# RWKV attention and SwiGLU block on one core: sign bits from the PSUM copy, a later third weights load, and units 2 and 3 in another order

## The chip, the cores and the metric

The kernel runs on one core of one Trainium2 chip. The metric is the time of one execution on the device in microseconds (us). The engines are PE (TensorE, matrix products), ACT (ScalarE), DVE (VectorE), POOL (GpSimd) and SP (SyncE, which issues most transfers). Each works through its own queue in order, and they wait for one another through semaphores. SBUF is the memory that engines and transfers share; PSUM is the small memory that PE writes its results into[...].

## The reference, cut to what matters

```
for t in range(S):                                   # rwkv5, B=4, H=8, S=768, D=48
    y[:, :, t] = r_t @ (state + u * k_t (x) v_t)
    state = w * state + k_t (x) v_t
x = y.transpose(0, 2, 1, 3).reshape(B * S, H * D)     # 3072 x 384
out = (silu(x @ w_gate) * (x @ w_val)) @ w_out        # d_ff = 1536
```

Here (x) is the outer product of a key and a value. The three weight matrices come in as 64-bit floats; everything else is fp32. The kernel therefore has to turn the weights into fp32 itself, by bit operations.

## The kernel before, in words

**Units.** The sequence is cut in 6 chunks of 128 steps. A chunk of one of the 4 batches is a unit, so there are 24 units; units 0 to 3 are the first chunks of the four batches. Within a unit the recurrence is a masked product of scores with v, plus a product with the state Z that came out of the earlier chunks.

A unit passes through these steps. `load(i)` brings k and r, `load_v(i)` brings v. `own_product(i)` and `own_sum(i)` (POOL, then DVE) form the diagonal term `du`. `turn(i)` transposes k and r on PE into a PSUM tile `tp`, and DVE (units 0 to 3, multiplying by a table of powers of w) or ACT (later units) copies it out as `kT` and `rT`. `diagonal(i)` writes `du` on the diagonal of `At`: four or eight blocks on ACT, the rest on POOL. `scores(i)` multiplies kT with rT on PE and DVE copies the part above the diagonal into `At` (COPY_PREDICATED, L386). `outputs(i)` forms `y_ps` on PE from At and v (and from Z, when the unit is not in the first chunk), and ACT copies it to `xT`. `update(i)` multiplies the scaled keys (`khat`, scaled by `scale_k` on POOL) with v on PE; for the first chunk DVE multiplies the result by w to the 128th, `w128`, into Z (L436).

**The block after it.** `gate_value(g, f)` computes 128 columns of the gate and of the value product for two units at a time: six matrix products into one PSUM tile `gv` (L450), the sigmoid on ACT (L456), and two products on DVE (L457, L458), the second of which writes `hT` and frees `gv`. There are two `gv` tiles. `project` multiplies hT with w_out. From the third pair of units on, other routines do both products with fewer matrix products; the change does not touch them.

**Weights.** They come in 18 chunks of 128 x 768 numbers, 768 KB each, in the order gate, value, gate, value, ..., then out. `load_weights` fetches the next chunk into one of three buffers `w_bits`; a number is a high and a low 32-bit word side by side. Rounding a chunk takes two halves. For each half, ACT reads the high words as fp32, takes the absolute value times 2 to the -112 (which moves the exponent) and writes it to PSUM as `w_mag` (`round_high`, L173). For the whole chunk ACT also scales the low words into `w_low` (`round_low`, L179; two buffers). DVE then does two operations for each half (`round_dve`): L188 takes the sign bit from the high words into the weight tile, and L189 shifts `w_mag` left by three and ORs it in. Last, POOL adds `w_low` (L199 for the halves of the first two chunks, L218 for whole chunks after that). `w_mag` has two places, `ps_w` and `ps_o`, one PSUM bank each, so a half can be prepared on ACT while DVE works on the other.

**What sets the order.** The program's order is the order of every engine's queue; nothing reorders it. The first part, units 0 to 3, is written out by hand after `flush()`; a loop over units from 4 on follows, with weights (`R`) and pieces of the feed-forward block (`F`) placed by the table `EARLY`. `feed(1)` emits the next piece whose weights are done. PSUM tiles of the attention part share four places (`ps_a`), taken in turn: a new tile waits until the tile four places before it has been read out. SP issues loads in the program's order too, and a load waits until the old contents of its buffer have been read.

Of the kernel before, what the change touches and what calls it, by code (L numbers as in the profile page):

```python
# [9 lines left out]
FP32 = mybir.dt.float32  # L10
INT32 = mybir.dt.int32
UINT32 = mybir.dt.uint32
AF = mybir.ActivationFunctionType
ALU = mybir.AluOpType
# [8 lines left out]
def fast(  # L23
# [44 lines left out]
    dve, pool, act, pe, sp = nc.vector, nc.gpsimd, nc.scalar, nc.tensor, nc.sync  # L68
# [6 lines left out]
    w128 = cst.tile([P, HP], FP32, name="w128")  # L75
# [41 lines left out]
    def load_v(i):  # L117
        c, b = divmod(i, B)
        rows = slice(P * c, P * (c + 1))
        for e in range(2):  # L120
            sp.dma_start(
                out=v_ld[i % 4][:, :, 64 * e : 64 * e + D],
                in_=v[b, :, rows, :].rearrange("(a e) t d -> e t a d", e=2)[e],
            )
# [14 lines left out]
    bits, mags, lows = {}, {}, {}  # L139
    done = {"load": 0, "act": 0, "pool": 0}  # L140

    def next_chunk(stage):
        n = done[stage]
        done[stage] = min(n + 1, NW)
        return n if n < NW else None

    def load_weights():
        n = next_chunk("load")
        if n is not None:
            src = chunks[n][0].bitcast(INT32)  # L150
            bits[n] = three.tile([P, WN, 2], INT32, name="w_bits", tag="w_bits")
            sp.dma_start(
                out=bits[n][:].rearrange("p (c f) two -> p c (f two)", c=src.shape[1]), in_=src
            )
# [6 lines left out]
    def halves(x, n):  # L161

        c = chunks[n][1].shape[1]
        x = x.rearrange("p (c f) -> p c f", c=c)
        f = x.shape[2]
        return [x[:, :, 0 : f // 2], x[:, :, f // 2 : f]] if c == 3 else [x[:, 0:1], x[:, 1:2]]

    def round_high(n, half, bank):
        hi = halves(bits[n][:, :, 1], n)[half]
        ps, tag = ((ps_w, "w_mag"), (ps_o, "o"))[bank]  # L170
        mag = ps.tile([P, WN // 2], INT32, name="w_mag", tag=tag)
        mags[n, half] = mag[:].rearrange("p (c f) -> p c f", c=hi.shape[1])
        act.activation(  # L173
            mags[n, half].bitcast(FP32), hi.bitcast(FP32), AF.Abs, scale=float(2.0**-112)
        )

    def round_low(n):
# [3 lines left out]
        )  # L181

    def round_dve(n, half):
        hi = halves(bits[n][:, :, 1], n)[half]
        f = hi.shape[2]
        dst = chunks[n][1].bitcast(INT32)
        dst = dst[:, :, half * f : half * f + f] if hi.shape[1] == 3 else dst[:, half : half + 1]
        dve.tensor_scalar(dst, hi, -(1 << 31), None, ALU.bitwise_and)  # L188
        dve.scalar_tensor_tensor(  # L189
            dst, mags.pop((n, half)), 3, dst, ALU.logical_shift_left, ALU.bitwise_or  # L190
        )

    def add_low(n, half):

        dst = chunks[n][1].bitcast(INT32)
        f = dst.shape[2] // 2
        cols = slice(half * f, half * f + f)
        low = lows[n][:].rearrange("p (c f) -> p c f", c=dst.shape[1])
        pool.tensor_tensor(dst[:, :, cols], dst[:, :, cols], low[:, :, cols], ALU.add)  # L199

    def round_act(next_load=1):
        n = next_chunk("act")
        if n is not None:
            round_high(n, 0, 0)
            round_low(n)
            round_dve(n, 0)
            round_high(n, 1, 1)
            round_dve(n, 1)
            del bits[n]
            for _ in range(next_load):  # L210
                load_weights()
# [15 lines left out]
    def own_product(i):  # L227
        kl, rl = raw(i)
        rk = two.tile([P, H, D], FP32, name="rk", tag="rk")[:]
        pool.tensor_mul(rk, rl, kl)  # L230
        pool.tensor_mul(rk, rk, ub[:])
        rks[i] = rk

    def own_sum(i):
        dus[i] = three.tile([P, H], FP32, name="du", tag="du")
        dve.tensor_reduce(dus[i][:], rks.pop(i), axis=AX.X, op=ALU.add)  # L236
# [39 lines left out]
    pw, pv = tables[:, 0, :, 0 : P + 1], tables[:, 1, :, 0:P]  # L276
    dve.memset(pw[:, :, P : P + 1], 1.0)
    dve.tensor_copy(pw[:, :, P - 1 : P], held[:].unsqueeze(2))
    for l in range(7):
        n = 1 << l  # L280
# [19 lines left out]
    def scale_k(i):  # L300
        pool.tensor_mul(khat[i % 4][:, :, 0:D], raw(i)[0], kscale[:])
# [4 lines left out]
    def natural_tables():  # L306
        for t, dst in ((pw[:, :, 1 : P + 1], kscale), (pv, rscale)):
            t_ps = ps_a.tile([P, HP, P], FP32, name="t_ps", tag="a")
            for a in range(HP):
                pe.transpose(t_ps[:, a, :], t[:, a, :], ident[:])  # L310
            act.copy(dst[:], t_ps[:].rearrange("p a (e x) -> p (a e) x", e=2)[:, :, 0:D])
# [5 lines left out]
    def diagonal(i):  # L317

        du = dus.pop(i)
        on_act = HP if i < 4 else H  # L320
        small.extend(
            lambda h=h: act.activation(  # L322
                At[i % 2][:, h, :], ident[:], AF.Identity, scale=du[:, h : h + 1]
            )
            for h in range(on_act)
        )
        if on_act < H:
            n = H - on_act
            pool.tensor_mul(
                At[i % 2][:, on_act:H], ident[:].unsqueeze(1).to_broadcast([P, n, P]),  # L330
                du[:, on_act:H].unsqueeze(2).to_broadcast([P, n, P]),
            )
# [4 lines left out]
    def turn(i):  # L337
        kr = khat[i % 4], rhat_of(i)
        tps = [ps_a.tile([P, HP, P], FP32, name="tp", tag="a") for _ in kr]
        turned[i] = three.tile([P, HP, P], FP32, name="rT", tag="rT")  # L340
        for tp, t, dst, table in zip(tps, kr, (kT[i % 2], turned[i]), (pw[:, :, 1 : P + 1], pv)):
            for a in range(HP):
                pe.transpose(tp[:, a, :], pair(t, a), ident[:])
            if i < 4:
                dve.tensor_mul(dst[:], tp[:], table)
            else:
                act.copy(dst[:], tp[:])
# [27 lines left out]
    def scores(i):  # L375

        ps = [ps_a.tile([P, HP, P], FP32, name="s_ps", tag="a") for _ in range(2)]
        for a in range(HP):
            for e in range(2):
                rows = slice(64 * e, 64 * e + D)  # L380
                pe.matmul(  # L381
                    ps[e][:, a, :], kT[i % 2][rows, at(i, a), :], turned[i][rows, at(i, a), :],
                    start=True, stop=True, skip_group_check=True,
                )
        for e in range(2):
            dve.copy_predicated(  # L386
                At[i % 2][:].rearrange("p (a e) t -> p a e t", e=2)[:, :, e],
                mask[:].bitcast(INT32).unsqueeze(1).to_broadcast([P, HP, P]), ps[e][:],
            )
# [27 lines left out]
    def update(i):  # L417
        c, b = divmod(i, B)
        if c == NCH - 1:
            return  # L420
        kh, vl, z = khat[i % 4], v_ld[i % 4], Z[b]
        ps = ps_a.tile([P, HP, D], FP32, name="u_ps", tag="a")
        for a in range(HP):
            for q in range(4):
                e, half = divmod(q, 2)
                pe.matmul(  # L426
                    ps[32 * q : 32 * q + 32, a, :], kh[:, 2 * a + e, 32 * half : 32 * half + 32],
                    vl[:, a, 64 * e : 64 * e + D],
                    start=True, stop=True, skip_group_check=True,
                )  # L430
        for e in range(2):
            rows = slice(64 * e, 64 * e + D)
            ze = z[rows, :, D * e : D * e + D]
            w = w128[rows].unsqueeze(2).to_broadcast([D, HP, D])
            if c == 0:
                dve.tensor_mul(ze, ps[rows], w)  # L436
            else:
                dve.tensor_add(ze, ps[rows], ze)
                pool.tensor_mul(ze, ze, w)
# [289 lines left out]

    turn(0)  # L730
    natural_tables()
    own_sum(0)
    diagonal(0)
    flush()
    own_product(1)
    load(2)
    load_weights()
    load_v(2)
    warm(3)
    turn(1)  # L740
    load(3)
    load_v(3)
    scores(0)
    own_sum(1)
    diagonal(1)
# [17 lines left out]
    for n in range(2):  # L763
        round_high(n, 1, n)
        round_dve(n, 1)
        add_low(n, 1)
        del bits[n], lows[n]
    done.update(act=2, pool=2)
    load_weights()
    turn(2)  # L770
    feed(1)
    own_sum(2)
    diagonal(2)
    flush()
    own_product(3)
    turn(3)
    dve.tensor_copy(w128[:].unsqueeze(2), pw[:, :, 0:1])
    scores(2)
    update(0)
    update(1)  # L780
    own_sum(3)
    diagonal(3)
    flush()
    scores(3)
    scale_k(2)
    outputs(2)
    load(4)
    round_act()
    feed(1)
    outputs(3)  # L790
    scale_k(3)
    round_act()
    round_pool()
    scale(4)
    load_v(4)
    feed(1)
    update(2)
    update(3)
    round_pool()
    own_product(4)  # L800
    load(5)
# [464 lines left out]
```

## Time and profile before

The median of 3 runs is 629.39 us (628.95 to 630.25). The profiled execution has a span of 627.9 us, with a PE clock of 1.00 in every stretch.

| what | us |
|---|---|
| span | 627.9 |
| PE busy | 611.4 |
| DVE busy | 366.8 |
| POOL busy | 300.1 |
| ACT busy | 239.5 |
| last rounding of weights on DVE starts | 104.8 |
| one L188 on DVE, shortest and longest | 0.35, 1.96 |
| one L189 on DVE | 0.56 |
| one L173 on ACT, median | 0.53 |

Busy time is an average over the whole span. A queue that is full in one stretch only is seen in the forty slices of the page (a digit is the busy share of a slice in tenths) and in the busy times by stretch. Who waited for whom is read from the list of waits, and when, from the order of time, where the number in brackets is the idle time ahead of an instruction and the name in it is what ended that idle time. "x" counts instructions; matrix products appear twice in these counts, since one fp32 product is run as two.

### The profile page before, as it was taken

The numbers are of one execution on the slowest core, as the hardware profiler recorded it, in microseconds if no ns is written. First come the engines' busy times: TensorE is split into PE (matmuls) and PEld (weight loads), VectorE is DVE, ScalarE is ACT, GpSimd is POOL, SyncE is SP. The second block draws the span as 40 slices with busy tenths as digits, with TensorE's granted clock in tenths as the row PEclk, the third lists the DMA queues.
The fourth block names the chain that finished last, engine by engine and source line by source line (L and its number), as shares of the span: only waits on it lengthen the run. The fifth ranks groups of instructions, "written<-read, shape, count | busy, mean of one in ns | idle before, by whom it ended". The sixth has DMA issues, their size and how long they took to land.

```text
span 627.9 us, 13037 instructions
## 1 busy us (share of the span) xinstructions
PE 611.4 (97%) x5040; PEld 550.5 (88%) x5040; DVE 366.8 (58%) x751; ACT 239.5 (38%) x647; POOL 300.1 (48%) x350
## 2 busy tenths in 40 slices
PE   8799999999999999999999999999999999999996
PEld 7588778899888899988899888899988899988896
DVE  6889999465556563466566355665345453355460
ACT  3368777321353512245330435432253321233310
POOL 5789778946648413563543635441433211443110
PEclk9999999999999999999999999999999999999999
DMA  8979873244341203322222402121000000000001
GB/s 191 246 169 243 219 242 94 40 72 80 73 69 24 45 12 66 76 47 45 40 37 57 92 12 37 25 42 41 27 2 1 1 1 26 27 0 1 1 2 55
DMA packets 138007, 40.47 MB, mean 64 GB/s; under 512 B 128592, under 2 KB 131792, under 8 KB 137936
## 3 DMA queue, kind: packets, MB, share of 16 engines
q1 hardware_dynamic: 134480, 34.82, 26.5%
q10 hardware_dynamic: 3456, 4.72, 2.1%
q8 instruction: 42, 0.69, 0.5%
q14 instruction: 29, 0.24, 0.1%
HBM read 28.51 MB, written 4.72 MB: 53 GB/s over the span
## 4 chain that ended last, share of the span: by engine, by line
PE 86%; DVE 7%; ACT 2%; DMA 2%; issue 1%; POOL 0%; DVEq 0%; ACTq 0%; POOLq 0%
PE c_b L627 25%; PE c_a L627 21%; PE o_f L521 13%; PE o_a L521 8%; PE o_b L521 6%; PE y_ps L411 5%; PE gv L450 4%; PE s_ps L381 3%; DVE At L386 1%; PE warm L265 1%; DMA hats<-in_r_dram 1%; DMA w_bits<-in_moe_w_out_dram 1%; DVE wg L188 1%; DVE wo L188 1%; PE u_ps L426 1%
## 5 line engine op out<-in xcount | busy, mean ns | idle before, releaser
L611 POOL TENSOR_TENSOR hT<-hT,u 128x256 f32<-128x256 f32 x60 | 46.9, 782 | 149.0 <-DVE hT L610 121.8
L634 ACT COPY u<-c_a 128x256 f32<-128x256 f32 x120 | 44.5, 371 | 85.8 <-PE c_a L627 83.5
L627 PE MATMUL c_a<-t,wv 128*128 128x256 f32 x240 | 72.0, 382 | 0.1
L627 PE MATMUL c_b<-xT,wg 128*128 128x256 f32 x240 | 71.6, 380 | 0.0
L607 ACT ACTIVATE sg<-hT 128x256 f32<-128x256 f32 x120 | 50.1, 417 | 52.5 <-DVE hT L636 33.8
L322 ACT ACTIVATE At<-ident,du 128x128 f32<-128x128 f32 x176 | 62.1, 398 | 16.2 <-DVE du L236 7.3
L627 PE MATMUL c_b<-xT,s 128*128 128x256 f32 x240 | 61.6, 379 | 0.0
L641 DVE TENSOR_TENSOR u<-u,c_b 128x256 f32<-128x256 f32 x60 | 25.1, 418 | 60.5 <-PE c_b L627 55.4
L627 PEld LDWEIGHTS c_b<-xT,s 128*128 128x128 f32 x240 | 45.2, 190 | 6.6 <-DVE u L641 0.2
L627 PEld LDWEIGHTS c_a<-t,wv 128*128 128x128 f32 x240 | 44.9, 190 | 6.9 <-ACT u L634 1.1
L627 PEld LDWEIGHTS c_b<-xT,wg 128*128 128x128 f32 x240 | 45.3, 190 | 6.0
L636 DVE TENSOR_TENSOR hT<-p,c_b 128x256 f32<-128x256 f32 x60 | 25.1, 419 | 41.6 <-PE c_b L627 38.6
L587 POOL TENSOR_TENSOR s<-wv,wg 128x256 f32<-128x256 f32 x24 | 17.6, 733 | 65.5 <-PE o_f L521 50.8
L386 DVE COPY_PREDICATED At<-mask,s_ps 128x512 f32<-128x512 int32 x48 | 32.9, 741 | 19.9 <-PE s_ps L381 12.4
L450 PE MATMUL gv<-xT,wg 128*128 128x256 f32 x144 | 36.9, 392 | 3.1 <-DVE hT L458 2.5
L304 POOL TENSOR_TENSOR hats<-r_ld,rscale 128x384 f32<-128x384 f32 x20 | 20.9, 1045 | 36.1 <-DMA v_ld<-in_v_dram 19.0
L639 DVE TENSOR_TENSOR hT<-hT,c_a 128x256 f32<-128x256 f32 x60 | 25.3, 421 | 19.8 <-PE c_a L627 18.4
L643 DVE TENSOR_TENSOR hT<-u,c_b 128x256 f32<-128x256 f32 x60 | 25.2, 421 | 19.8 <-PE c_b L627 19.6
L627 PE MATMUL c_b<-t,s 128*128 128x256 f32 x120 | 36.2, 383 | 0.3 <-DVE hT L636 0.3
L411 PE MATMUL y_ps<-At,v_ld 128*32 128x128 f32 x768 | 34.9, 273 | 1.4 <-DVE At L386 1.4
L627 PE MATMUL c_b<-xT,wv 128*128 128x256 f32 x120 | 35.9, 381 | 0.0
L627 PE MATMUL c_a<-t,s 128*128 128x256 f32 x120 | 35.8, 380 | 0.0
(135 smaller groups left out, 1394.6 us busy)
## 6 DMA issues: line engine op xcount, KB each, us to landing
hats<-hats SPq DMA_DIRECT2D x192, 32.0 KB, 2.0
w_bits<-in_moe_w_gate_dram SPq DMA_DIRECT2D x6, 768.0 KB, 6.5
v_ld<-in_v_dram SPq DMA_DIRECT2D x48, 96.0 KB, 3.4
w_bits<-in_moe_w_val_dram SPq DMA_DIRECT2D x6, 768.0 KB, 5.9
w_bits<-in_moe_w_out_dram SPq DMA_DIRECT2D x6, 768.0 KB, 6.0
out_dram<-o_sb ACTq DMA_DIRECT2D x24, 192.0 KB, 1.9
k_ld<-in_k_dram SPq DMA_DIRECT2D x20, 192.0 KB, 3.1
r_ld<-in_r_dram SPq DMA_DIRECT2D x20, 192.0 KB, 3.9
```

What stands on the lines that cost most here:

```text
L322: lambda h=h: act.activation(At[i % 2][:, h, :], ident[:], AF.Identity, scale=du[:, h : h + 1])
L386: dve.copy_predicated(At[i % 2][:].rearrange("p (a e) t -> p a e t", e=2)[:, :, e], mask[:].bitcast(INT32).unsqueeze(1).to_broadcast([P, H ...
L411: pe.matmul(ps[32 * q : 32 * q + 32, cc, :], *x, start=start, stop=stop, skip_group_check=True,)
L450: pe.matmul(gv[:, o, :].rearrange("p (i t) -> p i t", i=2), wt[:, c, P * f : P * (f + 1)], xT[:, 2 * g % NX : 2 * g % NX + 2, c, :], start ...
L521: pe.matmul(ps, lhs[:, f, :], rhs[:, f, :], start=(f == 0 and n in (0, 1, 4)), stop=(f == FH - 1), skip_group_check=True,)
L607: act.activation(x[what, f][:], h[j], AF.Sigmoid)
L611: pool.tensor_mul(h[1], h[1], x.pop(("u3", f))[:])
L627: pe.matmul(ps.rearrange("p (i t) -> p i t", i=2), lhs, rhs, start=first, stop=what not in ("p2", "p5", "p4", "p3"), skip_group_check=True,)
L634: act.copy(x[nm, f][:], ps)
L636: dve.tensor_add(h[0], x.pop(("p1", f))[:], ps)
L639: dve.tensor_mul(h[0], h[0], ps)
L643: dve.tensor_add(h[1], x.pop(("u2", f))[:], ps)
```

## The change

It has three parts.

1. The sign bit comes from PSUM. ACT copies the high words with their sign (`AF.Copy` in place of `AF.Abs`), so `w_mag` holds the sign as well, and both DVE operations read it. DVE no longer reads `w_bits`. Its purpose is to take one read of SBUF from DVE; in return the first of the two operations now has to wait for ACT's copy.
2. The third chunk of weights is fetched after k, r and v of unit 3 instead of ahead of v of unit 2, so that the unit's inputs come first.
3. The work of units 2 and 3 is put in another order. `turn(2)`, its diagonal, scores and `outputs(2)` come earlier, `turn(3)` comes after the scores of unit 2 and the updates of units 0 and 1, and the updates of units 2 and 3 stand right after `outputs(3)`. The copy of `w128` moves to the start, where the table of powers has just been made.

```
@@ round_high
         act.activation(
-            mags[n, half].bitcast(FP32), hi.bitcast(FP32), AF.Abs, scale=float(2.0**-112)
+            mags[n, half].bitcast(FP32), hi.bitcast(FP32), AF.Copy, scale=float(2.0**-112)
         )
@@ round_dve
-        hi = halves(bits[n][:, :, 1], n)[half]
+        hi = mags.pop((n, half))
...
         dve.tensor_scalar(dst, hi, -(1 << 31), None, ALU.bitwise_and)
-        dve.scalar_tensor_tensor(
-            dst, mags.pop((n, half)), 3, dst, ALU.logical_shift_left, ALU.bitwise_or
-        )
+        dve.scalar_tensor_tensor(dst, hi, 3, dst, ALU.logical_shift_left, ALU.bitwise_or)
@@ the order by hand
     natural_tables()
+    dve.tensor_copy(w128[:].unsqueeze(2), pw[:, :, 0:1])
     own_sum(0)
...
     load(2)
-    load_weights()
     load_v(2)
     warm(3)
     turn(1)
     load(3)
     load_v(3)
+    load_weights()
     scores(0)
...
         round_dve(n, 1)
+    turn(2)
+    own_sum(2)
+    diagonal(2)
+    for n in range(2):
         add_low(n, 1)
         del bits[n], lows[n]
     done.update(act=2, pool=2)
     load_weights()
-    turn(2)
     feed(1)
-    own_sum(2)
-    diagonal(2)
     flush()
-    own_product(3)
-    turn(3)
-    dve.tensor_copy(w128[:].unsqueeze(2), pw[:, :, 0:1])
     scores(2)
     update(0)
     update(1)
+    own_product(3)
+    turn(3)
+    outputs(2)
     own_sum(3)
     diagonal(3)
     flush()
     scores(3)
     scale_k(2)
-    outputs(2)
     load(4)
     round_act()
     feed(1)
     outputs(3)
     scale_k(3)
+    update(2)
+    update(3)
     round_act()
     round_pool()
     scale(4)
     load_v(4)
     feed(1)
-    update(2)
-    update(3)
     round_pool()
```

More of the change, by code (lines that the diff above doesn't have):

```diff
@@ L173, in round_high @@
         act.activation(
-            mags[n, half].bitcast(FP32), hi.bitcast(FP32), AF.Abs, scale=float(2.0**-112)
+            mags[n, half].bitcast(FP32), hi.bitcast(FP32), AF.Copy, scale=float(2.0**-112)
         )
@@ L183, in round_dve @@
     def round_dve(n, half):
-        hi = halves(bits[n][:, :, 1], n)[half]
+        hi = mags.pop((n, half))
         f = hi.shape[2]
@@ L188, in round_dve @@
         dve.tensor_scalar(dst, hi, -(1 << 31), None, ALU.bitwise_and)
-        dve.scalar_tensor_tensor(
-            dst, mags.pop((n, half)), 3, dst, ALU.logical_shift_left, ALU.bitwise_or
-        )
+        dve.scalar_tensor_tensor(dst, hi, 3, dst, ALU.logical_shift_left, ALU.bitwise_or)
     def add_low(n, half):
@@ L731, in fast @@
     natural_tables()
+    dve.tensor_copy(w128[:].unsqueeze(2), pw[:, :, 0:1])
     own_sum(0)
@@ L736, in fast @@
     load(2)
-    load_weights()
     load_v(2)
@@ L742, in fast @@
     load_v(3)
+    load_weights()
     scores(0)
@@ L765, in fast @@
         round_dve(n, 1)
+    turn(2)
+    own_sum(2)
+    diagonal(2)
+    for n in range(2):
         add_low(n, 1)
@@ L769, in fast @@
     load_weights()
-    turn(2)
     feed(1)
-    own_sum(2)
-    diagonal(2)
     flush()
-    own_product(3)
-    turn(3)
-    dve.tensor_copy(w128[:].unsqueeze(2), pw[:, :, 0:1])
     scores(2)
@@ L780, in fast @@
     update(1)
+    own_product(3)
+    turn(3)
+    outputs(2)
     own_sum(3)
@@ L785, in fast @@
     scale_k(2)
-    outputs(2)
     load(4)
@@ L791, in fast @@
     scale_k(3)
+    update(2)
+    update(3)
     round_act()
@@ L796, in fast @@
     feed(1)
-    update(2)
-    update(3)
     round_pool()
```

## The prediction, made before the changed kernel had run

> **What bounds the kernel now.** First the page: busy times and the forty slices.
>
> ```profile
> PE 611.4 (97%) x5040; PEld 550.5 (88%) x5040; DVE 366.8 (58%) x751; ACT 239.5 (38%) x647; POOL 300.1 (48%) x350
> PE   8799999999999999999999999999999999999996
> DVE  6889999465556563466566355665345453355460
> ```
>
> TensorE (PE) is busy nearly throughout, so the change can only win back PE's idle time: 627.9 - 611.4 = 16.5 us. VectorE (DVE) is full only in the first seven slices, where the weights are rounded. Next, what PE waited for from 9 to 110 us (columns: line, who ended the wait, us in total, times, longest):
>
> ```profile
> PE gv L450 <- DVE hT L458: 2.5, 3, 1.1
> PE y_ps L411 <- DVE At L386: 1.4, 2, 1.2
> PE y_ps L411 <- ACT kT L347: 1.0, 1, 1.0
> PE tp L343 <- DMA hats<-in_k_dram: 1.0, 1, 1.0
> PE tp L343 <- DMA hats<-in_r_dram: 0.8, 2, 0.5
> PE gv L450 <- ACT xT L415: 0.6, 1, 0.6
> PE s_ps L381 <- DVE At L386: 0.5, 1, 0.5
> ```
>
> That is 7.8 us. The same view after 110 us names one wait, 0.3 us: time saved before 110 us should reach the end. PE's order of time puts the three hT waits at 76.66, 90.12 and 102.92 us, the kT wait at 58.66, the DMA waits at 19.98, 24.20 and 25.33, the long At wait at 17.44 and the xT wait at 35.50. Third, the stretches between two outputs on PE (columns: stretch, then busy us and count of PE, PE's loads, DVE, ACT, POOL):
>
> ```profile
> 70.81:84.17 13.36, 12.38 (x150) 10.45 (x149) 12.56 (x24) 9.50 (x23) 10.86 (x10) 1.00 0.75 220
> 84.17:97.63 13.46, 12.38 (x149) 10.45 (x148) 12.32 (x25) 9.77 (x24) 11.08 (x10) 1.00 0.75 224
> ```
>
> A unit costs PE 12.38 us but takes 13.4: DVE sets that pace (92 to 94% busy, the rest almost all gaps between dependent instructions). Fourth, why DVE is slow, in order of time, GpSimd (POOL) first:
>
> ```profile
> 53.58 1.87 POOL L218 TENSOR_TENSOR wv<-wv,w_low 128x768 int32<-128x768 int32 x1
> 54.48 1.26 DVE L188 TENSOR_SCALAR wg<-w_bits 128x384 int32<-128x384 int32 x1
> 55.84 0.56 DVE L189 SCALAR_TENSOR_TENSOR wg<-w_mag,wg 128x384 int32<-128x384 int32 x1
> 56.31 0.41 DVE L188 TENSOR_SCALAR wv<-w_bits 128x384 int32<-128x384 int32 x1
> ```
>
> The first L188 ends 0.29 us after POOL's addition (53.58 + 1.87 = 55.45; 54.48 + 1.26 = 55.74); the second, with POOL idle at its start, takes 0.41. L189, which reads PSUM, takes 0.56 all 36 times. The 36 L188 sum to 28.0 us, mean 0.78; 17 of them are over 0.6.
>
> **What the Trainium skill says.** "SBUF — State Buffer", section Who interferes with whom: VectorE and GpSimd share a pair of SBUF ports, held for a whole instruction; tensor_scalar can take the pair, while an instruction with at most one SBUF input, outside the two-port modes, does not contend. "VectorE: DVE Perf Modes", section Why PSUM operands drop a tier: any PSUM operand caps fp32 at 1x and rules the two-port mode out. The trace agrees: L188 waits POOL out, L189 never does.
>
> **Part 1, the sign from PSUM.** L188 now reads w_mag in PSUM, 384 elements, and should no longer wait for POOL. Its new duration is not in the trace. Below: 0.41, its uncontended time now. Above: 0.56, L189's, same size with a PSUM operand. I take 0.55, because DVE's PSUM operations follow size (256 elements 0.42, 512 elements 0.68; the middle is 0.55). A pair L188+L189 costs duration + 0.10 to the next start + 0.48: before 0.78 + 0.58 = 1.36, after 1.13. From 52 us on the 24 L188 sum to 20.5 us, mean 0.85; after 24 x 0.55 = 13.2, saving 7.3 us of DVE. Per unit: DVE from the At copy at 74.41 to that at 87.88 is 13.47 us with six L188 of 4.81 us and a 0.46 wait; 13.47 - (4.81 - 3.30) - 0.46 = 11.5, under PE's 12.38. So PE sets the pace there and the three hT waits, 2.47 us, go. I leave 0.3 for in-order waits that remain.
>
> The added wait: L188 now waits for ScalarE's copy, where only L189 did. Where ScalarE is late, the 0.65 us from L188 to L189 moves behind it, and the whole DVE queue with it. It bites at 20 us: ScalarE's second-half copies follow xT at 19.50 and 19.97. Now L188 19.37, L189 20.06, kT of unit 2 at 21.53. After: L188 20.00, L189 20.65, L188 21.13, L189 21.78, kT 22.26, so 0.73 later. Copy in place of Abs: the w_mag row has the same size, taken at its 0.53; nothing. The bits buffer is now released by ScalarE's last read instead of DVE's; weight loads can be issued earlier, which only helps.
>
> **Part 2, the load order.** The third chunk (768 KB) goes behind v of unit 2 and k, r, v of unit 3. DMA moved 257 GB/s from 9 to 30 us, so k and r of unit 3 land about 3 us earlier (about 21 and 22 us) and stop mattering. The chunk was issued at 15.63 and will be near 22 or 23; landing took about 7 us, so about 29.5. ScalarE reads it at about 31 (below): hidden, with 1.5 us to spare.
>
> **Part 3, the order around units 2 and 3.** PE after: transposes of unit 2 and the first gate/value product until 23.2 as now; then scores(2), updates 0 and 1, transposes(3), y(2), scores(3). I walk it with trace durations. rT of unit 2 ends 23.5 (PE idles 0.35); scores 23.55 to 24.65; updates to 25.5. The diagonal: the row sum ends 24.0, ScalarE's four At 25.25, POOL's 25.1, so the At copy is 25.3 to 26.6. transposes(3) need its PSUM: 26.0 to 27.2 (idle 0.5). DVE: Z of units 0 and 1 26.6 to 28.0, kT and rT of unit 3 to 29.3. y(2) 27.4 to 28.5 (idle 0.2), scores(3) 29.3 to 30.4 (idle 0.8), gate/value 33.2, y(3) 34.3, updates 2 and 3 35.1, gate/value 35.1 to 37.9 (no xT wait: the updates fill it), next to 40.7. It ends at 41.80 now: 1.1 us gained. The copy of w128 (L777), 1.03 us while POOL works, moves to 10.8 us where POOL is idle and DVE waits anyway (0.67 before kT): nothing.
>
> What reaches the next stage is less. POOL runs without a pause from 35.98 to 55.45 in the trace. It starts when the third chunk's second L189 ends. After: At copy of unit 3 ends at 32.4 (33.3 now), two pairs to 34.7, so POOL starts 1.2 earlier. But Z of units 2 and 3 (1.47) now stand ahead of the fourth chunk's pairs: 34.7 + 0.8 (sg, hT) + 1.47 + 2.26 = 39.2, and POOL's second addition, at 39.85 now, starts at 39.2: 0.6 earlier. From there POOL sets the pace: w_low at 55.48 waits for POOL (its wait is in the trace), kT behind it frees the PSUM of y(4), the wait at 58.66. That wait stays. With some 0.3 from POOL no longer held up by L188 (its 1.82 us additions took up to 2.02), y(4) starts about 0.9 earlier, not 1.1.
>
> **Sum.** 0.9 by 58.66, plus 2.47 - 0.3 = 2.2 from the hT waits: 3.1 us. 629.4 - 3.1 = 626.3.
>
> **Rivals.** (A) POOL and ScalarE take over as the bound. For: POOL has 10.9 us of work in a unit of 12.38, w_low waits for it (1.44 at 75.41, 1.57 at 88.67), and now all of a rounding half waits for ScalarE. Against: POOL's 2.1 to 2.3 us idle once a unit is wait for DVE. If each of three units keeps 0.5: 3.1 + 0.3 - 1.5 = 1.9; with the start at 0.5 instead of 0.9, 1.5: 627.9. (B) More: DVE catches up before 58 us, so that wait goes too (1.0) and the start gives its full 1.1 with no residue (0.5 more): 4.6, so 624.8. Against: POOL's unbroken chain. (C) Slower: L188 is stalled by ScalarE often. With 0.35 us at each of 24 halves a pair is 1.48 against 0.85 + 0.58 = 1.43 now: 1.2 us more DVE where it is the bound; with the start 0.5 later (kT 0.73 late, nothing returned): 631.1. For: the 0.46 wait at 87.41 and that at 20 us. Against: these are the only two waits of L189 for ScalarE, 0.7 us in all, and ScalarE often waits for DVE instead (6.3 us).
>
> **Chances.** Forecast (625.4 to 627.2) 0.54, A (627.2 to 628.6) 0.23, B (below 625.4) 0.13, C and a return of all gains 0.10. Range 624.4 to 628.6: it leaves out C and the end of B. 0.2% is 1.26 us, a limit of 628.1; a little of A lies above it: faster 0.80, same 0.13, slower 0.07.
>
> **What would show it.** L188 all near 0.55, none over 0.7 (right); waits for ScalarE ahead of L188, near 20 us and few later; the hT waits of PE gone, units of 12.4 us between 58 and 110; the kT wait near 58 us still there, with w_low waiting for POOL; no DMA wait ahead of transposes(3). Wrong if L188 still follows POOL's ends, if PE shows new waits for the weights (wg, wv) or for w_low's successors, or if the third chunk lands after 31 us.

## The result, and the profile after

The changed kernel takes 625.9 us (median of 6 runs, 625.04 to 626.39) against 629.24 us before (6 runs); the ratio is 0.9944, with a 95% interval of 0.9931 to 0.9957. Measured twice more beside other kernels it came to 0.9936 (0.9922 to 0.9949) and 0.9937 (0.9923 to 0.9950). The profiled span went from 627.9 to 624.1 us.

Line numbers after the change are two lower than before for most of the code (L448 is the old L450), except L188 and L189, which keep theirs; POOL's long addition L218 is now L216.

First the page after: busy times and slices.

```profile
PE 610.6 (98%) x5040; PEld 550.9 (88%) x5040; DVE 358.1 (57%) x751; ACT 239.4 (38%) x647; POOL 297.3 (48%) x350
PE   8799999999999999999999999999999999999996
DVE  6878996373556574466575355574355463355460
```

DVE lost 8.7 us of busy time (366.8 to 358.1), nearly all of it L188: its 36 instructions take 19.9 us, against 28.0. PE's busy time hardly moved; what went is its idle time. The waits of PE from 9 to 110 us (line, who ended the wait, us in total, times, longest):

```profile
PE s_ps L379 <- DVE rT L343: 1.5, 2, 0.8
PE y_ps L409 <- issue: 1.2, 1, 1.2
PE y_ps L409 <- ACT kT L345: 0.8, 1, 0.8
PE tp L341 <- DVE At L384: 0.4, 1, 0.4
PE tp L341 <- POOL hats L299: 0.4, 1, 0.4
PE tp L341 <- POOL hats L302: 0.3, 1, 0.3
PE y_ps L409 <- DVE At L384: 0.2, 1, 0.2
```

The three waits for hT (2.5 us) are gone, and so are those for transfers (1.8) and for xT (0.6). New are the waits for rT of units 2 and 3 and, near 44.5 us, for POOL's scaling of unit 5. The wait for kT ahead of y of unit 4 shrank from 1.03 to 0.77. Next, two stretches between outputs on PE (stretch, then busy us and count of PE, PE's loads, DVE, ACT, POOL):

```profile
70.23:82.38 12.15, 12.15 (x150) 10.54 (x149) 10.99 (x24) 9.67 (x23) 10.79 (x10) 1.00 0.78 244
82.38:94.52 12.14, 12.14 (x149) 10.53 (x148) 11.47 (x24) 10.17 (x25) 10.50 (x10) 1.00 0.78 244
```

PE is busy without a break and a unit takes 12.15 us, not 13.4. DVE, at 90 to 94% of that, no longer sets the pace. Last, in order of time, an L188 that starts while POOL adds:

```profile
53.17 1.84 POOL L216 TENSOR_TENSOR wv<-wv,w_low 128x768 int32<-128x768 int32 x1
53.34 0.55 DVE L188 TENSOR_SCALAR wg<-w_mag 128x384 int32<-128x384 int32 x1
53.92 0.56 DVE L189 SCALAR_TENSOR_TENSOR wg<-w_mag,wg 128x384 int32<-128x384 int32 x1
```

It ends 1.1 us before POOL does. In the trace before, all 24 of the L188 that took longer than 0.42 us ended 0.21 to 0.29 us after an operation of POOL, and the other 12 took 0.35 to 0.42. After the change, the view of the line L188 (count, then shortest, median and longest in ns) has all 36 near 0.55, and it names the one new wait:

```profile
L188 DVE TENSOR_SCALAR wg<-w_mag x12: 542/547/558, 15.7 to 69.8; 128x384 int32<-128x384 int32 x12
L188 DVE TENSOR_SCALAR wv<-w_mag x12: 532/549/558, 18.2 to 74.5; 128x384 int32<-128x384 int32 x12
L188 DVE TENSOR_SCALAR wo<-w_mag x12: 547/558/559, 77.2 to 98.2; 128x384 int32<-128x384 int32 x12
...
  ACT w_mag L173: 2.5, 5
```

### The profile page after: what moved, and what is told of

Its sections match the earlier page's. It is cut to its first block, busy times and chain, and to the rows that moved or that the text cites. A ratio compares the mean times of both kernels' runs of the same rounds, so it can differ in the third digit from the quotient of the medians.

```text
span 624.1 us, 13011 instructions
## 1 busy us (share of the span) xinstructions
PE 610.6 (98%) x5040; PEld 550.9 (88%) x5040; DVE 358.1 (57%) x751; ACT 239.4 (38%) x647; POOL 297.3 (48%) x350
## 4 chain that ended last, share of the span: by engine, by line
PE 87%; POOL 4%; DVE 3%; SPq 2%; issue 1%; ACT 1%; DMA 1%; ACTq 0%; DVEq 0%; POOLq 0%
PE c_b L625 23%; PE c_a L625 19%; PE o_f L519 13%; PE o_a L519 8%; PE gv L448 7%; PE o_b L519 6%; PE y_ps L409 5%; PE s_ps L379 3%; SPq L356 2%; PE warm L263 1%; PE tp L341 1%; PE u_ps L424 1%; DMA r_ld<-in_r_dram 1%; POOL wv L216 1%; DVE At L384 1%
## 5 line engine op out<-in xcount | busy, mean ns | idle before, releaser
L448 PE MATMUL gv<-xT,wg 128*128 128x256 f32 x144 | 36.6, 390 | 0.0
L625 PE MATMUL c_a<-xT,wg 128*128 128x256 f32 x120 | 35.8, 380 | 0.0
```

Source lines behind the costliest of these rows:

```text
L448: pe.matmul(gv[:, o, :].rearrange("p (i t) -> p i t", i=2), wt[:, c, P * f : P * (f + 1)], xT[:, 2 * g % NX : 2 * g % NX + 2, c, :], start ...
L625: pe.matmul(ps.rearrange("p (i t) -> p i t", i=2), lhs, rhs, start=first, stop=what not in ("p2", "p5", "p4", "p3"), skip_group_check=True,)
```

## The experiments

Twelve runs in three groups of four follow. Each group ran on one chip beside the kernel before, which took 629.82 us in the first, 629.62 in the second and 630.20 in the third; the ratios of a group are to its own value. My theory: the loss was L188 waiting for the SBUF ports that POOL held; part 1 removes it and brings nearly everything; what the order at the start brings is set by POOL's chain. Rivals are named with each test.

**Part 1 alone.** The edit, on the kernel before:

```
-            mags[n, half].bitcast(FP32), hi.bitcast(FP32), AF.Abs, scale=float(2.0**-112)
+            mags[n, half].bitcast(FP32), hi.bitcast(FP32), AF.Copy, scale=float(2.0**-112)
...
-        hi = halves(bits[n][:, :, 1], n)[half]
+        hi = mags.pop((n, half))
```

> Part 1 alone: the sign from ScalarE's copy in PSUM, with the load order and the order of units 2 and 3 of before. Theory (part 1 carries nearly all): L188 at 0.55 us, units on PE of 12.15 us from 58 us on, the three hT waits of PE gone, about 3.2 us; at the start the late kT of unit 2 hides behind the wait for k and r of unit 3, so another 0.2 to 0.4. Time about 625.8, that is 3.4 us under the kernel before. Rival (the order is needed for it): with the old order DVE stays behind, two of three hT waits remain, and the time is about 628.

Measured: 625.93 us, ratio 0.9936 (0.9922 to 0.9949), which can't be told from the whole change (0.9936 to 0.9944, in other groups). The four longest waits of PE from 9 to 112 us:

```profile
PE tp L341 <- DMA hats<-in_k_dram: 2.2, 1, 2.2
PE y_ps L409 <- DVE At L384: 1.3, 2, 1.2
PE gv L448 <- ACT xT L413: 0.6, 1, 0.6
PE y_ps L409 <- ACT kT L345: 0.3, 1, 0.3
```

The old order's waits for transfers and for xT are still there, and no hT wait is. The rival, that the new order is needed to be rid of the hT waits, is out.

**Parts 2 and 3 alone.** The edit, on the changed kernel:

```
-        hi = mags.pop((n, half))
+        hi = halves(bits[n][:, :, 1], n)[half]
...
-        dve.scalar_tensor_tensor(dst, hi, 3, dst, ALU.logical_shift_left, ALU.bitwise_or)
+        dve.scalar_tensor_tensor(
+            dst, mags.pop((n, half)), 3, dst, ALU.logical_shift_left, ALU.bitwise_or
+        )
```

(and AF.Abs in place of AF.Copy again).

> Parts 2 and 3 alone: the new load order and the new order of units 2 and 3, with the sign read from SBUF as before. Theory: the DMA waits and the xT wait of PE near 24 to 36 us go, but POOL and DVE are no earlier at 39 us, L188 keeps its mean near 0.78 us and the hT waits stay. Time about 628.8, 0.4 us under the kernel before. Rival (the parts add up evenly): the order brings 1.5 us or more by itself, time about 627.6.

Measured: 629.13 us (21 runs), ratio 0.9989 (0.9978 to 0.9999): at most 0.2% faster, barely told from nothing. PE's order of time (start, us, in brackets the idle time ahead and who ended it):

```profile
58.69 0.43 PE L411 MATMUL y_ps<-rT,Z 112*32 112x128 f32 x8 [1.04 <-ACT kT L347]
76.73 1.53 PE L450 MATMUL gv<-xT,wg 128*128 128x256 f32 x6 [1.02 <-DVE hT L458]
89.85 1.53 PE L450 MATMUL gv<-xT,wg 128*128 128x256 f32 x6 [0.74 <-DVE hT L458]
102.98 1.53 PE L450 MATMUL gv<-xT,wg 128*128 128x256 f32 x6 [0.75 <-DVE hT L458]
```

y of unit 4 starts at 58.69, where the kernel before had 58.66: what the new order wins early is waited for again by then. POOL's second long addition starts no earlier either, at 39.86 (39.85 before). The hT waits stay.

**The load order undone.** The edit, on the changed kernel:

```
     load(2)
+    load_weights()
     load_v(2)
...
     load_v(3)
-    load_weights()
```

> The changed kernel with the third weights chunk loaded at its old place, ahead of v of unit 2. Theory: k and r of unit 3 land at about 24 and 25 us, before their transposes can start at 26.3 us, so nothing changes: 625.9, within 0.3. Rival (the load order matters): transposes of unit 3 wait for the transfers, and everything is 1 us later: 626.9.

Measured: 625.73 us, ratio 0.9932 (0.9918 to 0.9946). No difference. PE's order of time shows why:

```profile
26.17 1.28 PE L341 MATMUL tp<-ident,hats 128*128 128x128 f32 x8 [0.43 <-DVE At L384]
```

With the new order the transposes of unit 3 wait for the At copy of unit 2, which frees their PSUM, and no wait for their transfers is listed. Part 2 is hidden by part 3.

**The signs read from SBUF again, by an operation with a second operand in PSUM.** The edit, on the changed kernel; this kernel leaves out the right bits of the weights, as `w_mag` is ORed in unshifted as well:

```
-        dve.tensor_scalar(dst, hi, -(1 << 31), None, ALU.bitwise_and)
-        dve.scalar_tensor_tensor(dst, hi, 3, dst, ALU.logical_shift_left, ALU.bitwise_or)
+        dve.scalar_tensor_tensor(dst, hi, -(1 << 31), mag, ALU.bitwise_and, ALU.bitwise_or)
+        dve.scalar_tensor_tensor(dst, mag, 3, dst, ALU.logical_shift_left, ALU.bitwise_or)
```

Here `hi` is again the words of `w_bits` in SBUF, and `mag` is `w_mag` in PSUM.

> The changed kernel, but L188 is an operation with two tensors, the sign bits from w_bits in SBUF and w_mag in PSUM, in place of one with a constant only. The weights come out wrong in their low bits; the work is otherwise the same. Theory (the loss is the shared port, which this form does not take): L188 takes 0.56 us whatever POOL does, and the time is that of the changed kernel, 625.9 within 0.4. Rival (any read of the w_bits in SBUF beside POOL is slow): L188 is still held up to 1 to 2 us, and the time is near 628.5.

Measured: 625.44 us, ratio 0.9929 (0.9915 to 0.9942). L188 by tile:

```profile
L188 DVE SCALAR_TENSOR_TENSOR wg<-w_bits,w_mag x12: 531/544/555, 15.4 to 69.2; 128x384 int32<-128x384 int32 x12
L188 DVE SCALAR_TENSOR_TENSOR wv<-w_bits,w_mag x12: 542/546/561, 17.9 to 73.9; 128x384 int32<-128x384 int32 x12
L188 DVE SCALAR_TENSOR_TENSOR wo<-w_bits,w_mag x12: 544/548/554, 78.1 to 99.1; 128x384 int32<-128x384 int32 x12
```

So it was not any reading of SBUF beside POOL that was slow. A read of the same words by an operation with a second operand in PSUM is never held up, though 33 of the 36 run beside a busy POOL. The rival is out: the form of the operation decided. The edit changes two things in that form, the kind of operation and the second operand, and no run parts them. It puts out another rival too, that the gain comes from weight buffers which DVE no longer reads and so releases earlier: here DVE reads them again, and the time stays.

**The copy ahead of xT.** The one large new wait, 1.09 us of L188 at 20.39, is behind ScalarE's copy, which stood behind an xT that waits for PE. The edit, on the changed kernel:

```
     scale_k(1)
+    round_high(0, 1, 0)
     outputs(1)
     queue(0)
-    for n in range(2):
-        round_high(n, 1, n)
-        round_dve(n, 1)
+    round_dve(0, 1)
+    round_high(1, 1, 1)
+    round_dve(1, 1)
```

> The changed kernel, with ScalarE's copy of the second half of the first chunk placed ahead of its xT of unit 1, which waits for PE. Theory (the one costly added wait is L188 behind that copy, 1.09 us at 20.4 us): kT of unit 2 starts 0.8 to 1.1 earlier, PE's wait of 0.8 ahead of scores(2) goes, and all of it is handed on: about 0.8 off, 625.1. Rival (POOL's chain or the transfers take it up): under 0.3 off, 625.7.

Measured: 625.02 us, ratio 0.9935 (0.9921 to 0.9948), beside 625.59 and 0.9936 for the changed kernel. DVE's kT of unit 2, first in the changed kernel of that group, then here:

```profile
22.30 0.68 DVE L343 TENSOR_TENSOR kT<-tp,tables 128x512 f32<-128x512 f32 x1
```
```profile
21.32 0.68 DVE L343 TENSOR_TENSOR kT<-tp,tables 128x512 f32<-128x512 f32 x1
```

It is 1.0 us earlier, and nothing comes of it in these traces: the transposes of unit 3 start at 26.05 in both. In both, r of unit 2 landed late (PE waits 0.7 for it at 20.5 to 20.6), and by the end of the gate/value product behind those transposes kT and rT are there either way. My theory fell here. It is not shown that the added wait never costs anything: in the profiled run of the result r was in time, and PE waited 0.83 for rT of unit 2. The whole times decide nothing, as 0.6 us lies within their intervals.

**The rounding ahead of Z.** PE's order stays; in DVE's queue Z of units 2 and 3 goes behind the fourth chunk's rounding. The edit, on the changed kernel:

```
-    update(2)
-    update(3)
     round_act()
+    update(2)
+    update(3)
```

> The changed kernel, with the rounding of the fourth chunk ahead of Z of units 2 and 3 in DVE's queue; PE's order is the same. Theory (between 36 and 58 us POOL sets the pace, and Z in DVE's queue holds up its second long addition by 0.65): that addition starts at about 38.9 in place of 39.6, PE's waits near 44.5 us (0.7) nearly go, y of unit 4 starts 0.65 earlier, time about 625.3. Rival (PE or ScalarE sets the pace there): no difference, 625.9.

It ran a second time in the third group, and the changed kernel ran in both groups:

> Again the changed kernel with the rounding of the fourth chunk ahead of Z of units 2 and 3, for a second measure beside the changed kernel. Theory (POOL's pace): 0.6 under it, 625.1. Rival: no difference, 625.7.

> The changed kernel itself, beside the next three on one chip: 625.9, within 0.4. Both theories say the same.

> The changed kernel itself, beside the other three on one chip: 625.7, within 0.4. Both theories say the same.

Measured: 625.00 us, ratio 0.9931 (0.9918 to 0.9945), and, the second time, 624.97 us, ratio 0.9916 (0.9903 to 0.9930). The changed kernel beside them took 625.59 (0.9936) and 626.49 (0.9937). Both times it is the faster one, and both times the intervals overlap. The traces are clearer, if counted from the transposes of unit 3, since the start before them varies from run to run (last section). POOL's second long addition, first in the changed kernel of the second group (transposes at 26.05), then here (at 26.39):

```profile
39.32 1.83 POOL L216 TENSOR_TENSOR wv<-wv,w_low 128x768 int32<-128x768 int32 x1 [0.63 <-DVE wv L189]
```
```profile
39.00 1.84 POOL L216 TENSOR_TENSOR wv<-wv,w_low 128x768 int32<-128x768 int32 x1
```

From the transposes to the addition it is 13.27 and 12.61 us, and from the transposes to y of unit 4 31.74 (57.79 - 26.05) and 31.07 (57.46 - 26.39): 0.66 and 0.67 less, the whole of it handed on. The second run and the next experiment, which holds the same move, repeat it: y of unit 4 comes 31.13 and 31.04 us after the transposes, and 31.72 to 31.81 in the five traces of the changed kernel, of the old load order and of the copy ahead of xT. The rival, that PE or ScalarE sets the pace between, is out.

**Both moves together,** the copy ahead of xT and the rounding ahead of Z.

> The changed kernel with both moves together, the copy ahead of xT and the rounding ahead of Z. Theory (two separate links of one chain): the gains add, about 1.4 off, 624.5, faster than the changed kernel and the kernel before. Rival (the second link hides the first): 625.1.

Measured: 624.97 us, ratio 0.9925 (0.9912 to 0.9939). The sum of 1.4 is not there, as the copy's move brings nothing. Its profiled run had v of unit 0 land late (PE waits 2.15 us for it), so its trace can be read only from the transposes of unit 3 on, as above.

**POOL's queue refilled.** If POOL sets the pace, its two pauses, 2.0 us ahead of the first long addition and 0.65 ahead of the second, should be worth filling. The edit, on the changed kernel; all other queues stay as they are:

```
     round_act()
-    round_pool()
     scale(4)
+    round_pool()
     load_v(4)
     feed(1)
-    round_pool()
     own_product(4)
+    round_pool()
     load(5)
```

> The changed kernel with POOL's queue refilled: the scaling of unit 4 stands ahead of the third chunk's long addition, where POOL waits 2.0 us, and the own product of unit 4 ahead of the fourth chunk's, where it waits 0.65. PE, DVE and ScalarE keep their order. Theory (POOL sets the pace from 36 to 58 us): POOL's work for unit 5 starts 2 us earlier, PE's waits near 44.5 us (0.7) and ahead of y of unit 4 (0.75) go, 1.4 off: 624.3. Rival (ScalarE's own queue or the transfers of unit 5 hold y of unit 4): at most 0.5 off, 625.3.

Measured: 623.71 us, ratio 0.9899 (0.9884 to 0.9914), clear of the changed kernel's 0.9923 to 0.9950 in the same group: it is faster than both kernels. POOL's order of time:

```profile
33.24 1.01 POOL L299 TENSOR_TENSOR hats<-k_ld,kscale 128x384 f32<-128x384 f32 x1
34.21 1.02 POOL L302 TENSOR_TENSOR hats<-r_ld,rscale 128x384 f32<-128x384 f32 x1
35.34 1.83 POOL L216 TENSOR_TENSOR wg<-wg,w_low 128x768 int32<-128x768 int32 x1
37.13 1.00 POOL L228 TENSOR_TENSOR rk<-r_ld,k_ld 128x384 f32<-128x384 f32 x1
```

The scaling of unit 4 now sits where POOL waited. PE's waits near 44.5 us are gone, and y of unit 4 follows the transposes after 30.10 us (56.53 - 26.43) instead of 31.74: 1.64 less. What is left of its wait is 0.20. First y of unit 4 in the changed kernel of the second group, then here, and then the longest wait behind it, on ScalarE's queue, 1.96 us for the eighth weights chunk to land:

```profile
57.79 0.43 PE L409 MATMUL y_ps<-rT,Z 112*32 112x128 f32 x8 [0.74 <-ACT kT L345]
56.53 0.43 PE L409 MATMUL y_ps<-rT,Z 112*32 112x128 f32 x8 [0.20 <-ACT kT L345]
53.07 0.52 ACT L173 ACTIVATE w_mag<-w_bits 128x384 f32<-128x384 f32 x1 [1.96 <-DMA w_bits<-in_moe_w_val_dram]
```

In the group's medians the gain is 2.8 us (626.49 to 623.71); beyond the 1.6 it is not traced to a cause.

Count now from POOL's second long addition to y of unit 4. It is 18.81 and 18.83 us in the two kernels with the old L188, 18.44 to 18.52 in the ten traces with the new form of L188 and POOL's old order, and 16.80 here (56.53 - 39.73). In those ten the addition itself starts anywhere from 39.00 to 41.05: what moves it moves y by the same.

**POOL's queue refilled and the rounding ahead of Z.** The two edits together:

> The same, and the rounding of the fourth chunk ahead of Z of units 2 and 3 as well. Theory: PE's waits are gone already, so nothing is added: 624.3, the best so far and faster than both kernels. Rival: as for the run before it, with the 0.6 of the earlier test on top: 624.7.

Measured: 623.96 us, ratio 0.9902 (0.9887 to 0.9917). Nothing is added, as expected. In this trace ScalarE waits 2.92 us for that chunk, and y of unit 4 waits 1.15 for ScalarE's kT behind it, 18.29 us after POOL's second long addition, where it was 16.80 in the run before. So the transfer looks like the next bound of the stretch; no run tests it.

## Why the prediction was right, step by step

**The size of L188** was right: 0.55 taken, 0.53 to 0.56 measured, with no trace of POOL. The runs show that L188 was held up by POOL and is no longer. That a pair of ports is what held it is the Trainium skill's account ("SBUF — State Buffer", section Who interferes with whom); the traces agree with it and don't see the ports themselves. The two-operand test adds what the diff could not tell: the words may stay in SBUF, if the form of the operation is another. That a PSUM operand keeps it out ("VectorE: DVE Perf Modes", section Why PSUM operands drop a tier) agrees with all 36 L188 here.

**The hT waits** went, as forecast, and this term was mis-sized: 2.2 us forecast, 3.2 measured. The four stretches from y of unit 4 on took 12.15, 13.36, 13.46 and 12.80, together 51.77 us before, and 48.59 now. I had counted the waits alone (2.47) and held 0.3 back. A stop of PE costs more than the wait that is listed: 1.21 for 0.98, 1.31 for 1.08, 0.65 for 0.41, each time 0.23 or 0.24 more. The order-only kernel repeats it (units of 13.41, 13.12 and 13.13 for waits of 1.02, 0.74 and 0.75). The sign was in my own figures: I read PE's 12.38 us busy as what a unit needs, but the stretch from 58.66 to 70.81, which has no stop, already took 12.15. Nothing remained of the in-order waits that I had held 0.3 back for.

**The start** came out at 0.58 in the profiled runs (58.66 to 58.08), where 0.9 was forecast. In the run after, the 18 warm-up products at the start ended 0.34 later (9.48 against 9.14); less that, it is 0.92. Most links fit, 0.34 taken off each: kT of unit 2 at 22.18 (22.26 forecast), transposes of unit 3 at 25.93 (26.0), y(2) 27.36 (27.4), scores(3) 29.23 (29.3), POOL's two long additions 34.86 and 39.25 (34.7, 39.2), y of unit 4 57.74 (57.8). One does not: PE is done with the gate/value products at 40.10, where 40.7 was forecast, but that brings nothing, as PE then waits for POOL near 44.5. The 0.3 that I put down to POOL being held up less is there as well: from its second long addition to y of unit 4 it was 18.81 us before and is 18.49 now, and part 1 alone gives it (18.47); which link of part 1 does it was not tested. The step that Z of units 2 and 3 hold up POOL, so that 1.2 us becomes 0.6, is shown by moving Z; that POOL sets the pace to 58 us, by refilling its queue.

**Where the account was off.** The sum in the two terms is 0.92 + 3.18 - 0.34, or 3.8 in the span, and 3.3, 4.0 and 3.7 in the medians of the result and of the two repeats, for 3.1 forecast. That the first lay so near the forecast was partly luck, as the hT term was 1.0 too small; the span and the repeats lie 0.6 to 0.9 above the forecast. I gave most of the start to the new order. In whole time, part 1 alone has the same ratio, 0.9936, so parts 2 and 3 on top of it are not told from nothing: the load order because the transposes of unit 3 wait for an At copy anyway, and the rest because the start of a run varies by more than it could bring. The traces show 0.6 at y of unit 4 (58.41 with part 1 alone, 57.79 with all), but part 1 alone has one trace only. There as with the order alone, POOL's second long addition starts no earlier than before (39.94 and 39.86, for 39.85); only with both does it (39.59, and 39.32 in the second group).

**The rivals.** A (POOL and ScalarE take over) was half right: L188 does wait for ScalarE's copies (five times, 2.5 us) and w_low for POOL (5.0 us), yet past 58 us no such wait reaches PE. B did not come: the wait for kT near 58 us stayed, 0.77. C fell: past 58 us the added waits don't reach PE. The largest, at 20 us, hides behind a transfer where r of unit 2 is late; in the profiled run of the result it was not late, and PE waited 0.83 for rT there, for which the prediction had 0.35.

## What to carry to other kernels

When an operation's time in the trace is short alone and long beside another engine, and ends at a fixed distance from that engine's end, change the form or the place of an operand before moving work about. Then ask which engine runs without a pause ahead of the wait that is left, and fill the pauses that it has before that: two moved lines in POOL's queue brought 1.6 us of trace time, while a wait of 1.1 us removed from DVE, off the path in that trace, brought nothing. And price a stop of PE in such a row of products at more than the wait that is listed, here by 0.23 to 0.24 us.

## What the runs showed of the hardware that was not expected

A stop of PE in a row of 128x256 products cost 0.23 to 0.24 us beyond its listed wait, six times out of six.

The start varies between executions. The 18 warm-up products, always the same and always begun at 2.84 us or 2.85 us, took between 5.73 and 7.13 us in the profiled runs, and in some of them, not in others, PE waited for v of unit 0 (up to 2.15 us) or for r of unit 2 (up to 0.99). With the same code, transposes of unit 3 started at 26.05, 26.27 and 27.75 us. Small differences are therefore better read from a point behind the start than from whole times. What makes the start vary was not tested.
